# One pool for scores, value products and rows of reciprocals in an attention and gated-MLP kernel

## The chip, the cores and the metric

The kernel runs on one core of a Trainium2 chip. Its engines work side by side, each through its own list of instructions in a fixed order: TensorE (PE) multiplies matrices and is the only one that writes products, always into PSUM; VectorE (DVE) and ScalarE (ACT) read PSUM and compute elementwise; GpSimd (POOL) computes elementwise in SBUF; SyncE (SP) issues the transfers. PSUM has eight banks of 512 fp32 values per partition, and these banks are what the change hands out anew. The metric is the device time of one execution in microseconds (us).

## The reference

The kernel computes an attention with normalised queries and keys, and then a gated MLP over its result. There are 8 images, 12 heads, 448 positions and 64 values per head.

```python
q_n, k_n = rmsnorm(q, g_q), rmsnorm(k, g_k)
scores = q_n @ k_n.T / 8;  attn = exp(scores - max);  attn /= sum + 1e-9
x = (attn @ v)                                   # [8, 448, 768]
h = gelu_tanh(x @ w_in);  u, v = h[..., :512], h[..., 512:]
v_s = w_sg @ (layernorm(v) * g_ln) + b_sg        # mixes the 448 positions
out = x + (u * v_s) @ w_out
```

## The kernel before, in words

**Tiling.** Two heads form a pair, so an image has 6 pairs and the whole run has 48. Two pairs form a unit with one tile of queries and keys. Every factor of a product is held as a high and a low fp16 (or rounded fp32) part, and three products take the place of one.

**Scores (`scores`, L409).** A unit has 896 rows per head, cut into 7 tiles `s` of 128 rows, so a pair has three and a half. A tile has two banks, one per head, and comes from the pool `ps_s`, which holds two such tiles (`NS = 2`). TensorE fills it with six matmuls (twelve for the tile that the two pairs share, in half rows), L423. DVE takes the row maximum `nm` (L426), and ACT the two exponentials `ex` with their sums (L429), each of them an ACTIVATE and a read of the accumulator. With the second exponential the tile is free. The high part (ACT, L432) and the low part (DVE, L433) of the result go through a transposing transfer into `at`. The exact reciprocals of the sums are made in `recips`.

**Value product (`pv`, L445).** For each pair, `recip_row` (L392) first spreads the reciprocals over a row: 16 small matmuls into a tile `row` of the pool `ps_v`, which has a single bank (`NV = 1`), and a copy of it to SBUF by ACT (L406). Then 21 matmuls (L454, L459) build the product in the next tile `pv` of the same single bank, DVE multiplies it by the row in place (L461), ACT takes the high part `xh` (L464), and DVE the low part `xl` (L465), which is the last reader. So in `ps_v` the row's copy frees the bank for the product, and `xl` frees it for the next pair's row.

**MLP (`moe`, L489).** It runs one image behind, at lower priority. `mv` (L522, L525) makes the half that is normalised, `mu` (L580) the other half, `ms` (L608, L615) mixes positions, and `mo` (L647 to L659) adds the result to x. All their tiles come from `ps_m`, which has three banks (`NM = 3`). The gelus of a half run one after the other in a `cluster` (L471), since the gelu's table must be loaded (L475) and the exponential's restored afterwards (L484). Until a cluster runs, its tiles keep their banks, except those that ACT copies to SBUF first: `VC = (3,)` names the `mv` tile that is copied (L528, not in the first and last image), and `UC = (0, 1)` the two `mu` tiles (L585). The MLP of an image can start when its last pair's `xh` is there, and its remaining part is drained when the next one starts, one image later.

**Order.** The program is written as generators whose steps are interleaved with numbers (`SC`, `SV`, `M0`, `M1`, `MR`, `ML`), and with a priority per step; a scheduler then fixes the order on each engine, and which of a pool's slots a new tile takes (the one that it finds free, not strictly the next in turn). No order is decided on the chip.

Of the kernel before, what the change touches and what calls it, by code (L numbers as in the profile page):

```python
# [8 lines left out]
F32 = mybir.dt.float32  # L9
# [20 lines left out]

I0, WD = 5, 6

VC, UC = (3,), (0, 1)

SC, SV = 7, 3

NS, NV, NM = 2, 1, 3
NQK, NVR, RAWB = 2, 2, 3
NAT, NAH, NQT, NVH, HLB, GV = 3, 2, 2, 2, 3, 3
NOT, NX, NEX = 2, 12, 2  # L40
# [6 lines left out]
def kernel(  # L47
# [15 lines left out]
    B, H, S, D = q.shape  # L63
    P = 128
# [22 lines left out]
    sml = ctx.enter_context(tc.tile_pool(name="sml", bufs=4))  # L87
    xp = ctx.enter_context(tc.tile_pool(name="xp", bufs=NX))
    ps_s = ctx.enter_context(tc.tile_pool(name="ps_s", bufs=NS, space=bass.MemoryType.PSUM))
    ps_v = ctx.enter_context(tc.tile_pool(name="ps_v", bufs=NV, space=bass.MemoryType.PSUM))  # L90
    ps_m = ctx.enter_context(tc.tile_pool(name="ps_m", bufs=NM, space=bass.MemoryType.PSUM))
    mlp = None

# [295 lines left out]
        V.tensor_copy(out=rh, in_=y)  # L389
        V.tensor_tensor(out=rl, in0=y, in1=rh, op=ALU.subtract)  # L390

    def recip_row(i):  # L392

        u, j = divmod(i, NG)
        cs = slice(0, C4) if j == 0 else slice(CM, C7)
        rh, rl = U[u]["r", j]
        ps = ps_v.tile([P, 512], F32, name="row", tag="pv")[:, 0:S]
        for n, t in enumerate(range(cs.start, cs.stop)):
            ks, o = (slice(0, P), t * P - j * S) if t != CM else ((lo, SM), (hi, 0))[j]
            for rx in (rh, rl):  # L400
                for h in range(2):
                    w = ks.stop - ks.start
                    mm(out=ps[h * HP:(h + 1) * HP, o:o + w], lhsT=rx[ks, 2 * n + h:2 * n + h + 1].broadcast_to([w, HP]),  # L403
                       rhs=ident_h[ks, ks], start=(n == 0 and rx is rh), stop=(n == CM and rx is rl), skip_group_check=True)
        row = att.tile([P, S], F32, name="row", bufs=1)
        A.activation(out=row, in_=ps, func=AF.Copy)  # L406
        return row
# [37 lines left out]
    def pv(i):  # L445
        r = R[i]
        vh, vl = r["vh"], r["vl"]
        o = i % NAT * S
        yield
        row = recip_row(i)  # L450
        ps = ps_v.tile([P, 512], F32, name="pv")[:, 0:S]
        parts = ((vh, 0), (vl, 0), (vh, C7))
        for k_, (vx, n) in enumerate(parts):
            mm(out=ps, lhsT=vx[:, CM:CM + 2].rearrange("p c d -> p (c d)"), rhs=at_all[:, n + CM, o:o + S],  # L454
               start=(k_ == 0), stop=False, skip_group_check=True)
        for c in range(CM):
            for vx, n in parts:
                for h in range(2):
                    mm(out=ps[h * HP:(h + 1) * HP], lhsT=vx[:, c + h * (C4 + 1)], rhs=at_all[:, n + c + h * C4, o:o + S],  # L459
                       start=False, stop=(c == CM - 1 and n == C7), skip_group_check=True)  # L460
        V.tensor_tensor(out=ps, in0=ps, in1=row, op=ALU.mult)  # L461
        xh = xp.tile([P, S], F16, name="xh")
        xl = xp.tile([P, S], F16, name="xl")
        A.activation(out=xh, in_=ps, func=AF.Copy)  # L464
        V.tensor_tensor(out=xl, in0=ps, in1=xh, op=ALU.subtract)  # L465
        XT[i] = (xh, xl)
        del R[i]
        yield
# [245 lines left out]
    for i in range(NI + 1):  # L714
# [30 lines left out]
        if i > 0:  # L745
            streams.append((pv(i - 1), SV))
# [60 lines left out]
```

## Time and profile before

| | |
|---|---|
| time, 3 runs | 1026.87, 1028.56 (median), 1028.88 us |
| profiled execution: span from first to last instruction | 1021.5 us |
| median less span (what lies around the span) | 7.1 us |
| PE, DVE, ACT busy | 826.5, 801.4, 739.6 us |
| granted TensorE clock, mean | 0.925 |

The profile gives for the profiled execution its span alone; the 7.1 us around it are the difference to the median. Busy time is the union of an engine's instructions. A row of a group reads: line, engine, operation, out<-in, shapes, count, then busy time in us and the mean of one in ns, then the idle time ahead of it and who ended it. A row of waits reads: who waited, for whom, us in total, times, longest. A row of the timeline or of the chain of waits begins with its start and its length in us.

### The profile page before, as it was taken

Reading aid. Unit: us, or ns where it says so; the run is one execution under the profiler, and the core shown is the slowest. Engines: PE = TensorE matmul, PEld = TensorE weight load, DVE = VectorE, ACT = ScalarE, POOL = GpSimd, SP = SyncE. Lnnn points to the kernel's source line nnn. Section 1 sums busy time; section 2 is a strip of 40 time slices with the busy share of each in tenths; the row PEclk is TensorE's granted clock in tenths of the full one; section 3 lists DMA queues with packets and bytes.
Section 4 is the critical chain, followed back from the end, with each engine's and each line's share of the span. In section 5 each row is a group of like instructions: output and inputs, shape, how many; then the busy total and the mean of one; then the engine's idle time right before and its main releaser. Section 6 shows DMA issues by size and latency. Waiting matters only on the chain.

```text
span 1021.5 us, 16315 instructions
## 1 busy us (share of the span) xinstructions
PE 826.5 (81%) x5700; PEld 423.3 (41%) x5700; DVE 801.4 (78%) x1476; ACT 739.6 (72%) x1449; POOL 385.4 (38%) x263
## 2 busy tenths in 40 slices
PE   0324467737788899789897999989997899999998
PEld 0111224312553346344453455434643365445546
DVE  5699998999979977888789977887789768776140
ACT  2766798766777878686886877688778877786241
POOL 1465820436734362341543146322453253004021
PEclk9986678868989999899999899999998999999999
DMA  6977677776498869786789749793797676844102
GB/s 158 229 197 174 143 179 164 170 171 120 114 189 192 183 137 194 162 202 127 136 202 190 169 105 200 177 206 84 161 203 167 126 149 158 163 91 102 36 1 63
DMA packets 448002, 155.68 MB, mean 152 GB/s; under 512 B 404336, under 2 KB 441776, under 8 KB 447920
## 3 DMA queue, kind: packets, MB, share of 16 engines
q1 hardware_dynamic: 447344, 154.18, 69.3%
q8 instruction: 45, 0.74, 0.3%
q10 hardware_dynamic: 576, 0.46, 0.2%
q14 instruction: 37, 0.30, 0.1%
HBM read 43.57 MB, written 11.01 MB: 53 GB/s over the span
## 4 chain that ended last, share of the span: by engine, by line
DVE 31%; PE 28%; ACT 16%; DMA 10%; issue 9%; POOL 3%; SPq 3%; ACTq 0%; DVEq 0%; POOLq 0%
DVE ahl L433 8%; DMA at<-ahl 5%; DVE nm L426 5%; ACT ex L429 5%; ACT ahl L432 3%; PE s L423 3%; PE pv L459 3%; DVE vl L375 2%; DMA vr<-in_v_dram 2%; DVE ss L314 2%; DVE vl L568 1%; ACT sqv L358 1%; DVE pv L461 1%; DMA raw<-in_moe_w_in_dram 1%; SPq L302 1%
## 5 line engine op out<-in xcount | busy, mean ns | idle before, releaser
L429 ACT ACTIVATE ex<-s,nm 128x448 f32<-128x448 f32 x336 | 209.4, 631 | 76.8 <-DVE nm L426 51.6
L433 DVE TENSOR_TENSOR ahl<-ex,ahl 128x896 f16<-128x896 f32 x168 | 213.4, 1272 | 56.8 <-ACT ahl L432 55.4
L423 PE MATMUL s<-qt 64*128 64x448 f16 (+1 forms) x1152 | 156.9, 389 | 88.7 <-ACT ex L429 62.4
L426 DVE TENSOR_REDUCE nm<-s 128x2 f32<-128x896 f32 x168 | 180.8, 1081 | 18.4 <-PE s L423 18.2
L432 ACT ACTIVATE ahl<-ex 128x896 f16<-128x896 f32 x168 | 159.7, 951 | 37.8 <-DMA at<-ahl 35.8
L335 POOL TENSOR_TENSOR qk<-qk,ny 128x896 f32<-128x896 f32 x46 | 85.7, 1885 | 139.1 <-DVE ny L125 109.2
L619 POOL TENSOR_TENSOR gt<-gt,u 128x448 f32<-128x448 f32 x32 | 39.1, 1224 | 239.8 <-DVE gt L618 181.7
L340 POOL TENSOR_TENSOR hl<-qk,hl 128x896 f16<-128x896 f32 x46 | 94.6, 2070 | 69.9 <-ACT hl L339 69.7
L423 PEld LDWEIGHTS <-qt 64*128 64x128 f16 (+1 forms) x1152 | 49.2, 102 | 163.9 <-issue 102.8
L459 PE MATMUL pv<-at,vh 128*64 128x448 f16 x576 | 91.8, 371 | 0.0
L580 PEld LDWEIGHTS <-wi 128*128 128x128 f16 x576 | 57.6, 104 | 72.6 <-issue 31.3
L334 POOL TENSOR_TENSOR qk<-qk,gg 128x896 f32<-128x896 f32 x23 | 50.2, 2181 | 80.4 <-ACT sqk L313 78.2
L403 PE MATMUL row<-ident_h,rh 128*64 128x128 f16 (+1 forms) x384 | 36.6, 241 | 39.9 <-DVE xl L465 30.4
L429 ACT ACTIVATION_READ_ACCUMULATOR ex<-s,nm 128x1 f32 x336 | 67.8, 202 | 0.0
L314 DVE TENSOR_REDUCE ss<-sqk 128x14 f32<-128x896 f32 x48 | 51.6, 1076 | 17.6 <-ACT sqk L313 17.6
L313 ACT ACTIVATE sqk<-qk 128x896 f32<-128x896 f32 x48 | 45.6, 951 | 18.6 <-DVE ss L314 10.3
L339 ACT ACTIVATE hl<-qk 128x896 f16<-128x896 f32 x48 | 44.6, 945 | 13.6 <-POOL qk L335 6.9
L459 PE MATMUL pv<-at,vl 128*64 128x448 f16 x288 | 53.2, 367 | 0.0
L375 DVE SCALAR_TENSOR_TENSOR vl<-vr,v_s,vh 128x512 f16<-128x512 f32 x48 | 49.7, 1039 | 1.3 <-ACT vh L374 1.0
L459 PEld LDWEIGHTS <-vh 128*64 128x64 f16 x576 | 33.7, 114 | 40.5 <-issue 23.4
L403 PEld LDWEIGHTS <-rh 128*64 128x64 f16 (+1 forms) x384 | 22.5, 117 | 61.9 <-DVE xl L465 34.6
L522 PEld LDWEIGHTS <-xh 128*128 128x128 f16 x288 | 25.9, 99 | 46.8 <-issue 13.0
(1100 smaller groups left out, 2063.7 us busy)
## 6 DMA issues: line engine op xcount, KB each, us to landing
out_dram<-ot SPq DMA_DIRECT2D x56, 192.0 KB, 3.0
vr<-in_v_dram SPq DMA_DIRECT2D x32, 192.0 KB, 3.4
raw<-in_moe_w_in_dram SPq DMA_DIRECT2D x12, 512.0 KB, 5.5
qk<-in_q_dram SPq DMA_DIRECT2D x47, 128.0 KB, 2.9
qk<-in_k_dram SPq DMA_DIRECT2D x47, 128.0 KB, 2.8
vr<-in_v_dram SPq DMA_DIRECT2D x32, 144.0 KB, 3.2
qk<-in_q_dram SPq DMA_DIRECT2D x47, 96.0 KB, 2.6
qk<-in_k_dram SPq DMA_DIRECT2D x47, 96.0 KB, 2.6
```

The source lines that it names most:

```text
L314: V.tensor_reduce(out=SS[u][:, x], in_=skv, axis=AX.X, op=ALU.add)
L335: E.tensor_tensor(out=qk, in0=qk, in1=r["rs"][:, x * SSW:(x + 1) * SSW].unsqueeze(2).broadcast_to([P, SSW, D]), op=ALU.mult)
L340: E.tensor_tensor(out=l_, in0=r["qk"][:, x], in1=h_, op=ALU.subtract)
L375: V.scalar_tensor_tensor(out=vl.rearrange("p c d -> p (c d)"), in0=vr, scalar=sc, in1=vf, op0=ALU.mult, op1=ALU.subtract)
L403: mm(out=ps[h * HP:(h + 1) * HP, o:o + w], lhsT=rx[ks, 2 * n + h:2 * n + h + 1].broadcast_to([w, HP]), rhs=ident_h[ks, ks], start=(n == 0 ...
L423: mm(out=ps[r_, h, 0:S], lhsT=qt[hs, qx, t * P + r_.start:t * P + r_.stop], rhs=qt[hs, kx, j * S:(j + 1) * S], start=(m == 0), stop=(m == 2))
L426: V.tensor_reduce(out=nm, in_=ps[:, :, 0:S], axis=AX.X, op=ALU.max, negate=True)
L429: A.activation(out=ex[:, h], in_=ps[:, h, 0:S], func=AF.Exp, bias=nm[:, h:h + 1], accum_out=sums[:, t, h:h + 1])
L432: A.activation(out=ahl[:, 0], in_=ex, func=AF.Copy)
L433: V.tensor_tensor(out=ahl[:, 1], in0=ex, in1=ahl[:, 0], op=ALU.subtract)
L459: mm(out=ps[h * HP:(h + 1) * HP], lhsT=vx[:, c + h * (C4 + 1)], rhs=at_all[:, n + c + h * C4, o:o + S], start=False, stop=(c == CM - 1 and ...
L580: done = mm(out=ps[:, 0:S], lhsT=ww[:, g, f * P:(f + 1) * P], rhs=xx, start=(n == 0), stop=(n == 17))
```

## The change

The pool `ps_v` goes. A pair's `pv` tile now comes from `ps_s` under the scores' tag, as a tile of two banks: the product in the first, the row of reciprocals in the second. `ps_s` still holds two tiles. The bank that `ps_v` had goes to `ps_m`, which now has four. The copies of the `mv` tile (`VC`, six images) and of the second `mu` tile (`UC`, eight images) go. Lines after L90 stand one to two lines higher in the changed kernel (L423 is L421 there, L429 is L427, L589 is L588).

```diff
-VC, UC = (3,), (0, 1)
+VC, UC = (), (0,)
-NS, NV, NM = 2, 1, 3
+NS, NM = 2, 4
-    ps_v = ctx.enter_context(tc.tile_pool(name="ps_v", bufs=NV, space=bass.MemoryType.PSUM))
-    def recip_row(i):
+    def recip_row(i, ps):
         ...
-        ps = ps_v.tile([P, 512], F32, name="row", tag="pv")[:, 0:S]
         ...
-        row = recip_row(i)
-        ps = ps_v.tile([P, 512], F32, name="pv")[:, 0:S]
+        ps2 = ps_s.tile([P, 2, 512], F32, name="pv", tag="s")
+        ps = ps2[:, 0, 0:S]
+        row = recip_row(i, ps2[:, 1, 0:S])
```

The scheduler makes a new order of it on every engine. Three places follow; numbers behind a name tell one tile from the next, and "..." stands for matmuls that only repeat the row above and for weight loads.

**TensorE, between the last matmuls of one image's MLP and the first of the next image's (fifth MLP to sixth).** Before, the last `mo` matmuls, the score tiles and the first `mv` matmuls stand mixed:

```order
L659 MATMUL mo__7903<-wo_h_259,gl_7537 128x384
L403 MATMUL row_8168<-ident_h_89,rh_8089 64x64
...
L659 MATMUL mo__7903<-wo_h_259,gh_7493 128x384
L659 MATMUL mo__7903<-wo_l_260,gh_7493 128x384
L659 MATMUL mo__7903<-wo_h_259,gl_7639 128x384
...
L423 MATMUL s_8214<-qt_7714 128x448
...
L423 MATMUL s_8230<-qt_7714 64x448
...
L525 MATMUL mv__8289<-wi_256,xh_7096 64x256
```

In the changed kernel six score tiles and a whole pair's row and product stand there with no MLP matmul among them:

```order
L658 MATMUL mo__7857<-wo_h_256,gl_7594 128x384
L421 MATMUL s_7702<-qt_7146 128x448
...
L421 MATMUL s_7741<-qt_7146 128x448
...
L401 MATMUL pv_7777<-ident_h_86,rh_7650 64x64
...
L421 MATMUL s_7838<-qt_7146 128x448
...
L453 MATMUL pv_7777<-at_100,vh_7421 128x448
...
L421 MATMUL s_7881<-qt_7146 64x448
...
L421 MATMUL s_7947<-qt_7146 128x448
...
L421 MATMUL s_7963<-qt_7146 128x448
L131 MATMUL psc_8069<-vpart_7942,ones_79 128x2
...
L524 MATMUL mv__8241<-wi_253,xh_7054 64x256
```

What moved: two score tiles with MLP work on both sides became six tiles and a product in a row. Of the two slots, `pv_7777` has one from its first row matmul on, and `s_7741`, `s_7838` and `s_7881` follow one another in the other.

**ACT in the same stretch of the changed kernel**, from the first tile's exponentials to the last tile's (two exponentials are one row with x2):

```order
L427 ACTIVATE ex_7711,sums_7701<-s_7702,nm_7709 128x448 x2
L427 ACTIVATE ex_7750,sums_7701<-s_7741,nm_7748 128x448 x2
L404 ACTIVATE row_7794<-pv_7777 128x448
L427 ACTIVATE ex_7847,sums_7701<-s_7838,nm_7845 128x448 x2
L373 ACTIVATE vh_7934<-vr1_95,v_s_6756 128x512
L463 ACTIVATE xh_7818<-pv_7777 128x448
L427 ACTIVATE ex_7896,sums_7701<-s_7881,nm_7894 128x448 x2
L357 ACTIVATE sqv_7945,vpart_7942<-vr1_95 128x1536
L338 ACTIVATE hl_8050<-qk_7158 128x2x7x64
L427 ACTIVATE ex_7956,sums_7701<-s_7947,nm_7954 128x448 x2
L312 ACTIVATE sqk_8213<-qk_7681 128x896
L427 ACTIVATE ex_7972,sums_7701<-s_7963,nm_7970 128x448 x2
```

Four splits `ahl` and a second `hl` stand between these rows as well. ACT has all of its usual work for these tiles there, in a stretch in which TensorE has no MLP work.

**ACT, the first image's cluster of the `u` half.** Before, it stands in one piece:

```order
L475 ACT_TABLE_LOAD
L589 ACTIVATE u_1764<-mu__2030,hs_1099 128x448
L589 ACTIVATE u_1761<-u_1761,hs_1099 128x448
L589 ACTIVATE u_1762<-u_1762,hs_1099 128x448
L589 ACTIVATE u_1763<-mu__1977,hs_1099 128x448
L484 ACT_TABLE_LOAD
```

In the changed kernel exponentials have come between, and each change of table is a load:

```order
L474 ACT_TABLE_LOAD
L427 ACT_TABLE_LOAD
L427 ACTIVATE ex_1850,sums_1840<-s_1841,nm_1848 128x448 x2
...
L588 ACT_TABLE_LOAD
L588 ACTIVATE u_1754<-mu__2018,hs_1092 128x448
L588 ACTIVATE u_1752<-mu__1881,hs_1092 128x448
...
L427 ACT_TABLE_LOAD
L427 ACTIVATE ex_1981,sums_1840<-s_1972,nm_1979 128x448 x2
...
L588 ACT_TABLE_LOAD
L588 ACTIVATE u_1751<-u_1751,hs_1092 128x448
L588 ACTIVATE u_1753<-mu__1965,hs_1092 128x448
L483 ACT_TABLE_LOAD
```

What moved: the cluster has six table loads where it had two. The clusters of the other images stand in one piece in both.

## The prediction

> **What bounds the kernel now.** First the busy time of each engine by stage, then who waits inside the long middle stage, then one pair's timeline. Columns of the stage table: stretch, its length, busy time of PE, PE's weight loads, DVE, ACT and POOL, granted TensorE clock, DMA share, GB/s.
>
> ```profile
> 0.00:120.00 120.00, 35.31 (x247) 14.81 (x251) 97.89 (x156) 71.82 (x145) 63.00 (x47) 0.84 0.75 183
> 120.00:330.00 210.00, 152.53 (x1008) 75.12 (x1001) 189.14 (x346) 162.93 (x310) 92.84 (x59) 0.82 0.73 161
> 330.00:930.00 600.00, 552.24 (x3893) 278.23 (x3891) 492.59 (x926) 470.15 (x935) 214.27 (x141) 0.97 0.75 160
> 930.00:1022.00 92.00, 86.45 (x559) 55.12 (x559) 21.78 (x51) 34.72 (x62) 15.32 (x17) 1.00 0.19 46
> ```
>
> Up to 330 us DVE is the fullest engine (189.1 of 210 us). From 330 to 930 us, where two thirds of the pairs run, it is TensorE: 552.2 of 600 us, so 47.8 us idle. The tail is TensorE's too. No TensorE work goes with the change, so the middle can win at most those 47.8 us, and it loses whatever new idle time TensorE gets. Its waits there, and below them those over the whole run:
>
> ```profile
> PE s L423 <- ACT ex L429: 11.2, 13, 1.7
> PE row L403 <- DVE xl L465: 7.5, 5, 3.3
> PE pv L454 <- ACT row L406: 4.5, 4, 2.1
> PE ms__8822 L608 <- ACT u L589: 2.7, 1, 2.7
> PE mu__8508 L580 <- ACT vg L508: 2.5, 1, 2.5
> ...
> PE row L403 <- DVE xl L465: 30.4, 11, 8.9
> PE pv L454 <- ACT row L406: 5.6, 6, 2.1
> ```
>
> Waits for PSUM by the attention are 11.2 + 7.5 + 4.5 = 23.2 us of the 47.8. The score pool is not short today: each wait for `ex` averages 11.2 / 13 = 0.9 us. One pair (`s` tile, row, copy, product, its three readers):
>
> ```profile
> 576.12 0.74 PE L423 MATMUL s<-qt 64*128 64x448 f16 x6
> 578.04 0.25 PE L403 MATMUL row<-ident_h,rh 128*64 128x128 f16 x2
> 579.97 0.54 ACT L406 ACTIVATE row<-row 128x448 f32<-128x448 f32 x1
> 583.15 0.36 PE L454 MATMUL pv<-at,vh 128*128 128x448 f16 x1
> 587.38 0.63 DVE L461 TENSOR_TENSOR pv<-pv,row 128x448 f32<-128x448 f32 x1
> 590.57 0.62 DVE L465 TENSOR_TENSOR xl<-pv,xh 128x448 f16<-128x448 f32 x1
> ```
>
> From the first row matmul to the end of `xl` are 591.2 - 578.0 = 13.2 us. Today that occupies a bank of its own; in the change it occupies one of the scores' two slots.
>
> **The change part by part.** *Copies and tables.* Gone are six copies of 128x256 and eight of 128x448; added are four table loads in the first image's cluster, by the order.
>
> ```profile
> L528 ACT ACTIVATE vg<-mv__8289 x1: 366/366/366, 761.4 to 761.4; 128x256 f32<-128x256 f32 x1
> L585 ACT ACTIVATE u<-mu__5928 x1: 544/544/544, 575.1 to 575.1; 128x448 f32<-128x448 f32 x1
> L475 ACT ACT_TABLE_LOAD x18 | 23.1, 1283 | 16.2 <-PE mv__10601 L522 8.9 <-PE mv__10824 L522 2.2 <-PE mu__10958 L580 1.9
> ```
>
> 6 x 0.37 + 8 x 0.54 = 6.5 us go, 4 x 1.28 = 5.1 us come. ACT is idle a fifth of the time, which hides both: 0. Without that cover it would be -1.4.
>
> *A fourth MLP bank.* Before, three `mv` tiles wait in three banks with the fourth copied out; after, four wait in four. When the gelus start, every bank is taken in both, so the waits `mu <- vg` and `ms <- u` stay. Only `mo` gets a bank to spare, and no wait of the middle stage of any size names it. 0; at best the two waits quoted, 5.2 us.
>
> *The row's own bank.* The product no longer waits for the row's copy, nor the row for the last pair's `xl`: -4.5 - 7.5 = -12 in the middle. Of the early remainder (30.4 + 5.6 - 12.0 = 24.0) I take a tenth, TensorE not being the bound there: -2. Bounds 0 and -24. The copy itself still comes ahead of the multiplication and is now one reader among DVE's and ACT's others.
>
> *Two slots for three and a half score tiles and a product per pair.* The built program shows which slot each tile takes, so one can read off how much TensorE work stands between a tile's last matmul and the matmul that takes the slot over. That work must last longer than the readers. Their durations, with those of what else ACT does between:
>
> ```profile
> L426 DVE TENSOR_REDUCE nm<-s 128x2 f32<-128x896 f32 x168 | 180.8, 1081 | 18.4 <-PE s L423 18.2
> L429 ACT ACTIVATE ex<-s,nm 128x448 f32<-128x448 f32 x336 | 209.4, 631 | 76.8 <-DVE nm L426 51.6
> L429 ACT ACTIVATION_READ_ACCUMULATOR ex<-s,nm 128x1 f32 x336 | 67.8, 202 | 0.0
> L432 ACT ACTIVATE ahl<-ex 128x896 f16<-128x896 f32 x168 | 159.7, 951 | 37.8 <-DMA at<-ahl 35.8
> L433 DVE TENSOR_TENSOR ahl<-ex,ahl 128x896 f16<-128x896 f32 x168 | 213.4, 1272 | 56.8 <-ACT ahl L432 55.4
> L313 ACT ACTIVATE sqk<-qk 128x896 f32<-128x896 f32 x48 | 45.6, 951 | 18.6 <-DVE ss L314 10.3
> L339 ACT ACTIVATE hl<-qk 128x896 f16<-128x896 f32 x48 | 44.6, 945 | 13.6 <-POOL qk L335 6.9
> L358 ACT ACTIVATE sqv<-vr 128x1536 bf16<-128x1536 f32 x16 | 23.7, 1482 | 6.4 <-DMA vr<-in_v_dram 4.9 <-DVE ss L314 1.1 <-DVE nx L322 0.4
> L374 ACT ACTIVATE vh<-vr,v_s 128x512 f16<-128x512 f32 x48 | 33.8, 714 | 7.1 <-PE pv L459 6.5 <-DVE v_s L141 0.6
> L461 DVE TENSOR_TENSOR pv<-pv,row 128x448 f32<-128x448 f32 x48 | 30.0, 624 | 16.5 <-PE pv L459 16.4
> L464 ACT ACTIVATE xh<-pv 128x448 f16<-128x448 f32 x48 | 25.9, 539 | 20.0 <-DVE pv L461 19.9
> L465 DVE TENSOR_TENSOR xl<-pv,xh 128x448 f16<-128x448 f32 x48 | 29.4, 612 | 1.5 <-ACT xh L464 1.5
> ...
> 568.15 0.57 PE pv L454 x3
> 568.71 1.82 PE pv L459 x18
> 619.97 2.18 PE mo__6416 L659 x12
> 624.79 0.70 PE row L403 x16
> ```
>
> With nothing in their way the readers of a score tile need 1.08 + 2 x (0.63 + 0.20) = 2.75 us, those of a product 0.62 + 0.54 + 0.61 = 1.78 us. By the order of before, no tile of the middle has less than that as cover. By the new order 31 have, and 22 of them stand in five stretches, one at each passage from one image's MLP to the next, in which TensorE has no MLP matmul left: 4, 6, 4, 6 and 4 score tiles with a row and a product. The second of the long ones is the stretch shown above. Its seven slots are taken over after 1.42, 1.42, 0.74, 0.70, 2.39, 1.48 and 0.74 us of TensorE work (0.74 a score tile, 1.48 the shared one, 0.70 the row, 2.39 the product, 0.7 the four `mo` matmuls left at 2.18 / 12 each), against 1.78, 2.75, 2.75, 2.75, 2.75, 1.78 and 2.75 needed: 8.4 us short. The five together are 24.5 us short, by the bare durations: the floor. With one other instruction of the length of `ahl` on DVE (1.27 us) ahead of a score tile's readers and two ahead of a product's, 4.0 and 4.3 us, they are 63.6 us short: the ceiling. (In the pair above, the product ends at 583.15 + 2.39 = 585.5 and `xl` at 591.2, 5.7 us later, with TensorE busy meanwhile and in no hurry.)
>
> A second count lies between. From the first tile's exponentials to the last tile's ACT has, in the long stretch, 10 x 0.83 + 4 x 0.95 (`ahl`) + 2 x 0.95 (`hl`) + 0.95 (`sqk`) + 1.68 (`sqv` and its accumulator, taken as 0.19) + 0.54 (the row) + 0.54 (`xh`) + 0.71 (`vh`) = 18.4 us, TensorE 7.5 us: 10.9 idle. The five make 43 us. ACT may enter a stretch ahead by about the 2.75 us of a tile's readers, five times: 43 - 14 = 29. I take **+30**, near this count.
>
> Outside these stretches nine tiles are 9.5 us short by bare durations, and 29.7 us is the ceiling; MLP matmuls stand near them, so I take +8.
>
> *The clock after idle time.* A wait of TensorE already costs more than its length: after 1.5 us of it the eighteen matmuls of one tile took 6.3 us, at a clock of 0.53, where the same eighteen take 3.4.
>
> ```profile
> 561.80 0.53 PE L580 MATMUL mu__5814<-xh,wi 128*128 128x448 f16 x1 [1.54 <-ACT vg L508]
> 557.00:568.00 11.00, 9.06 (x48) 3.60 (x43) 10.54 (x25) 10.37 (x18) 2.21 (x2) 0.53 0.74 178
> ...
> 561.80 6.34 PE mu__5814 L580 x18
> 683.78 3.43 PE mu__7295 L580 x18
> ```
>
> That is 2.9 us. One such dip at each of the five stretches would cost 14; I take half, **+7**, bounds 0 and 14, since the matmuls there are few. The Trainium skill, "TensorE: Matmul & The Clock Gate", Part 1, says that the clock falls to half after about one idle window of 3.4 us and returns after a busy one. That rule speaks against the change, since every stretch without MLP work is a row of short idle times; the trace agrees on the half rate (0.53) but shows it around a wait of 1.5 us. By the rule each stretch would bring its dip, and the sum would be +38.
>
> **Sum.** 0 + 0 - 14 + 30 + 8 + 7 = +31. Span 1021.5 + 31 = 1052.5; with the 7.1 us around it **1060 us**, 3% more.
>
> **The rivals.** *(B) The scores become slot-bound throughout.* If the readers queue at DVE and ACT as they do now, the ceilings hold: 63.6 + 29.7 + 14 - 14 = +93, 1122 us. For it: DVE is busy 82% and ACT 78% of the middle. Against: while TensorE stands still their queues empty. It decides from the point where ACT or DVE has more than one foreign instruction ahead of a slot's readers.
>
> *(C) Faster.* The mechanism: TensorE reaches each stretch late, with ACT and DVE idle ahead of it, and the stretch is no longer than the idle time that TensorE has today in the same image (47.8 us over five and a half images). It decides if the stretches replace that idle time in place of adding to it: then the 23.2 us of slot waits go, and a tenth to a half of the early 24. -2 to -12 there, -12 to -23 here: -14 to -35, some 1004 us at -25. Against it: the floor of 24.5 us holds even with ACT and DVE idle.
>
> *(D) No change worth the name.* The floor, no dips, and nothing outside: +24.5, less 14, and 5 from the MLP banks: +5; a little more gain early makes it 0, 1029 us.
>
> In all of these the first 330 us may shift by 10 us either way, since the product now holds a slot through the long waits for DVE there; that is taken into the range alone.
>
> **How the numbers follow.** Forecast 0.50 (its own range 1036 to 1088), B 0.12, C 0.23, D 0.15. 0.2% is 2 us, about what a measurement of this kernel tells from none. D gives 0.08 to no change, 0.05 to slower, 0.02 to faster: faster 0.25, same 0.08, slower 0.67. The range 1008 to 1090 leaves out most of B and the lower half of C.
>
> **What would show it.** In the changed kernel: TensorE idle in the middle near 80 us; a larger `s <- ex` and a new `s <- xl` in its waits, near 40 us together, at five places some 110 us apart; no `pv <- row` wait; a granted clock there below 0.97; six table loads in the first `u` cluster. I am wrong if TensorE's idle time does not grow, or if it grows outside these five places.

## The result, and the profile after

| | before | change |
|---|---|---|
| time, median | 1028.72 us (4 runs, 1026.87 to 1031.21) | 1112.84 us (4 runs, 1110.07 to 1116.32) |
| ratio | 1 | 1.0843, 95% interval 1.0794 to 1.0891 |
| profiled execution, span | 1021.5 us | 1114.1 us |
| granted TensorE clock, mean | 0.925 | 0.876 |

The change makes the kernel 8.4% slower: 84 us, where 31 were forecast; the time lies above the range. The two profiled executions differ by 92.6 us, some 8 more than the medians. Runs for which time and span are both known have 1.7 to 2.5 us around the span, so the profiled execution of before took about 1023.4 us, and most of the 7.1 us that the section on the kernel before puts around the span are the distance of that execution from the median. The profiled execution of the change is the slowest of its four. The breakdowns below go by the profiles, and their total is too large by these 8 us. The stage table of the changed kernel, with the columns of the prediction's first fence:

```profile
0.00:120.00 120.00, 37.11 (x215) 14.62 (x215) 95.80 (x149) 67.70 (x136) 72.01 (x51) 0.79 0.74 180
120.00:330.00 210.00, 149.13 (x940) 68.63 (x940) 177.13 (x326) 158.15 (x293) 88.42 (x55) 0.78 0.66 154
330.00:930.00 600.00, 501.99 (x3450) 258.18 (x3451) 452.93 (x823) 420.19 (x819) 195.57 (x129) 0.89 0.66 144
930.00:1114.00 184.00, 160.96 (x1097) 86.09 (x1094) 96.03 (x180) 100.29 (x194) 30.69 (x29) 0.98 0.39 85
```

From 330 to 930 us TensorE ends 3450 matmuls where it ended 3893, and DVE and ACT are less busy too. No engine is fuller there than before; the time has gone into waits. What TensorE waits for in that stretch of the changed kernel (who, for whom, us in total, times, longest), and below "..." the same over the whole run, with the largest of the kernel before as the last row:

```profile
PE s L421 <- DVE xl L464: 24.4, 10, 5.3
PE pv L401 <- ACT ex L427: 18.7, 8, 4.0
PE psc L131 <- ACT sqv L357: 10.6, 5, 4.4
PE s L421 <- ACT ex L427: 6.6, 7, 1.6
PE pv L453 <- ACT row L404: 3.3, 4, 1.0
...
PE s L421 <- ACT ex L427: 42.9, 22, 5.2
PE pv L401 <- ACT ex L427: 42.7, 18, 7.3
PE s L421 <- DVE xl L464: 39.5, 15, 8.4
PE pv L453 <- ACT row L404: 6.2, 8, 1.0
...
PE s L423 <- ACT ex L429: 62.4, 30, 7.7
```

Two of these waits did not exist before: a score tile waits for the last reader of a product (`s <- xl`), and a product's row waits for the exponentials of a score tile (`pv L401 <- ex`). Over the run they are 39.5 + 42.7 = 82 us. But `s <- ex` fell from 62.4 to 42.9 us, and `row <- xl`, 30.4 us before, is gone. Together with `pv <- row` these waits grew from 98.4 to 131.3 us, by 33 us only.

For the comparison of kernels with other spans I cut each run at work instead of at times: *early* ends with the `xl` of the 13th pair, *middle* with that of the 47th (34 pairs), and the *tail* is the rest, to the end of the span. The middle of before and of the change, as rows of the stage table:

```profile
334.90:942.50 607.60, 559.84 (x3962) 284.39 (x3961) 496.47 (x929) 475.25 (x947) 214.62 (x144) 0.97 0.75 158
```

```profile
357.20:1049.40 692.20, 583.95 (x4056) 299.27 (x4055) 511.07 (x909) 478.17 (x941) 210.10 (x143) 0.90 0.64 140
```

So the 92.6 us are: early 357.2 - 334.9 = +22; middle +84.6, of it TensorE idle 108.2 - 47.8 = +60 and busy +24; tail 64.7 - 79.0 = -14. Of the 24, some 95 matmuls that were in the tail before are about 13 us at 0.141 us each, and the other 11 go with the slower clock (0.90 against 0.97). Of the 60, waits of scores, rows and products for a slot or for the row's copy are 38 (60.9 us against 23.2), and another 10.6 is `psc` (sums of squares that scale v) waiting for ACT's squares (0.2 us before). In the early part the same waits did not grow (75.2 us before, 70.5 in the change); TensorE is 18 us longer busy there, at a lower clock and with 40 more matmuls, and idle for 4 us more. DVE, the fullest engine of that part, is idle for 59 us where it was for 43. What makes it wait is not traced.

One of the five forecast stretches, the third, on TensorE ("..." stands for rows left out):

```profile
657.62 0.74 PE L421 MATMUL s<-qt 64*128 64x448 f16 x6 [0.16 <-ACT ex L427]
658.43 0.35 PE L453 MATMUL pv<-at,vh 128*128 128x448 f16 x1
...
660.91 0.76 PE L421 MATMUL s<-qt 64*64 64x448 f16 x12
665.22 1.49 PE L421 MATMUL s<-qt 64*128 64x448 f16 x12 [3.54 <-DVE xl L464]
669.88 0.32 PE L401 MATMUL pv<-ident_h,rh 128*64 128x128 f16 x2 [3.17 <-ACT ex L427]
```

The shared tile at 660.91 takes one slot, the product has the other, and TensorE stands still for 3.5 us until `xl` gives it back; two score tiles take both slots, and the next product waits 3.2 us for `ex`. That is the picture that the prediction drew. All five, with TensorE's busy time and the granted clock:

```profile
399.50:412.10 12.60, 7.33 (x72) 3.77 (x72) 7.48 (x17) 8.65 (x20) 0.00 (x0) 0.93 0.84 192
520.10:541.70 21.60, 12.74 (x105) 5.84 (x101) 12.63 (x18) 11.65 (x26) 0.00 (x0) 0.84 0.87 187
654.70:670.20 15.50, 8.55 (x87) 4.77 (x85) 12.11 (x18) 11.24 (x26) 0.00 (x0) 0.87 0.95 194
770.80:792.50 21.70, 12.61 (x87) 5.03 (x83) 13.53 (x19) 12.92 (x28) 0.00 (x0) 0.69 0.88 181
903.50:920.90 17.40, 9.66 (x86) 4.96 (x87) 12.14 (x19) 11.66 (x28) 0.00 (x0) 0.84 0.78 170
```

Length less busy time: 5.3 + 8.9 + 7.0 + 9.1 + 7.7 = 38 us. That leaves 108.2 - 38 = 70 us of idle time outside them, 22 more than before had in its whole middle. Of the 24.4 us of `s <- xl` above 22.5 lie in the five stretches; of the 18.7 us of `pv <- ex` only 7.2 do.

### The profile page after: what moved, and what is told of

The parts are those of the page before. It is cut to its first block, busy times and chain, and to the rows that moved or that the text cites. A ratio compares the mean times of both kernels' runs of the same rounds, so it can differ in the third digit from the quotient of the medians.

```text
span 1114.1 us, 16296 instructions
## 1 busy us (share of the span) xinstructions
PE 849.2 (76%) x5700; PEld 427.5 (38%) x5700; DVE 821.9 (74%) x1476; ACT 746.3 (67%) x1439; POOL 386.7 (35%) x263
## 4 chain that ended last, share of the span: by engine, by line
PE 33%; DVE 26%; ACT 16%; issue 9%; DMA 9%; SPq 3%; POOL 2%; ACTq 0%; DVEq 0%; POOLq 0%
DVE ahl L431 5%; DVE nm L424 5%; ACT ex L427 4%; PE pv L458 4%; DMA at<-ahl 3%; PE s L421 3%; DVE vl L374 2%; ACT ahl L430 2%; DMA vr<-in_v_dram 2%; DVE ss L313 2%; ACT L474 2%; PE pv L453 1%; DMA qk<-in_k_dram 1%; SPq L277 1%; POOL qk L334 1%
## 5 line engine op out<-in xcount | busy, mean ns | idle before, releaser
L427 ACT ACTIVATE ex<-s,nm 128x448 f32<-128x448 f32 x336 | 208.9, 628 | 125.3 <-DVE nm L424 116.5
L431 DVE TENSOR_TENSOR ahl<-ex,ahl 128x896 f16<-128x896 f32 x168 | 204.2, 1218 | 88.3 <-ACT ahl L430 87.9
L421 PE MATMUL s<-qt 64*128 64x448 f16 (+1 forms) x1152 | 148.2, 403 | 105.3 <-ACT ex L427 42.9
L339 POOL TENSOR_TENSOR hl<-qk,hl 128x896 f16<-128x896 f32 x46 | 97.3, 2126 | 295.7 <-ACT hl L338 295.6
L421 PEld LDWEIGHTS <-qt 64*128 64x128 f16 (+1 forms) x1152 | 46.8, 104 | 180.9 <-issue 70.6
L458 PE MATMUL pv<-at,vh 128*64 128x448 f16 x576 | 102.3, 412 | 0.0
L401 PE MATMUL pv<-ident_h,rh 128*64 128x128 f16 (+1 forms) x384 | 35.6, 239 | 53.3 <-ACT ex L427 42.7
L427 ACT ACTIVATION_READ_ACCUMULATOR ex<-s,nm 128x1 f32 x336 | 66.5, 198 | 0.0
L373 ACT ACTIVATE vh<-vr,v_s 128x512 f16<-128x512 f32 x48 | 34.3, 716 | 44.5 <-PE pv L458 44.5
L453 PE MATMUL pv<-at,vh 128*128 128x448 f16 x96 | 39.7, 413 | 30.5 <-DMA at<-ahl 15.8
L458 PE MATMUL pv<-at,vl 128*64 128x448 f16 x288 | 59.1, 408 | 0.0
L312 ACT ACTIVATE sqk<-qk 128x896 f32<-128x896 f32 x48 | 45.4, 945 | 16.1 <-DVE ss L313 8.5
L458 PEld LDWEIGHTS <-vh 128*64 128x64 f16 x576 | 36.6, 125 | 48.8 <-issue 35.4
L401 PEld LDWEIGHTS <-rh 128*64 128x64 f16 (+1 forms) x384 | 24.4, 117 | 72.8 <-issue 38.9
```

What stands on the lines that cost most here:

```text
L339: E.tensor_tensor(out=l_, in0=r["qk"][:, x], in1=h_, op=ALU.subtract)
L421: mm(out=ps[r_, h, 0:S], lhsT=qt[hs, qx, t * P + r_.start:t * P + r_.stop], rhs=qt[hs, kx, j * S:(j + 1) * S], start=(m == 0), stop=(m == 2))
L427: A.activation(out=ex[:, h], in_=ps[:, h, 0:S], func=AF.Exp, bias=nm[:, h:h + 1], accum_out=sums[:, t, h:h + 1])
L431: V.tensor_tensor(out=ahl[:, 1], in0=ex, in1=ahl[:, 0], op=ALU.subtract)
```

## The experiments

Three theories are tested. **S**: a product keeps one of the two slots for long, and the scores suffer in step with it. **O**: the loss is on the MLP's side, in the banks and the copies. **K**: taking turns costs by itself, however short the product's stay. The table gives what all runs showed; the ratio is to the kernel before on the same chip, and so the column to compare by. "Hold" is the mean time for which a product keeps its score slot, from the first matmul in it to the end of its last reader, in the 34 pairs of the middle, worked out from the starts and ends of these instructions.

| run | slots | MLP banks | median us | ratio (95%) | early / middle / tail us | idle TensorE, middle | hold |
|---|---|---|---|---|---|---|---|
| before | 2, product apart | 3 | 1028.7 | 1 | 335 / 607.6 / 79 | 48 | - |
| change | 2 shared | 4 | 1112.8 | 1.084 (1.079-1.089) | 357 / 692.2 / 65 | 108 | 11.9 |
| share_only | 2 shared | 3 | 1135.9 | 1.107 (1.103-1.111) | 358 / 707.0 / 66 | 110 | 13.6 |
| share_bank4 | 2 shared | 4 | 1107.6 | 1.080 (1.075-1.085) | 363 / 675.8 / 65 | 98 | 11.2 |
| after_sbuf | 2 shared | 4 | 1104.1 | 1.076 (1.073-1.080) | 351 / 683.5 / 66 | 95 | 10.8 |
| before_sbuf | 2, product apart | 3 | 1041.9 | 1.016 (1.011-1.021) | 343 / 613.3 / 80 | 51 | - |
| row_apart | 2 shared | 4, row in one | 1121.5 | 1.095 (1.089-1.100) | 358 / 697.3 / 69 | 111 | 7.5 |
| own_two | 2, product apart | 2 | 1046.8 | 1.021 (1.016-1.026) | 329 / 633.8 / 85 | 65 | - |
| before_m2 | 2, product apart | 2 | 1045.3 | 1.020 (1.015-1.024) | 328 / 630.9 / 85 | 69 | - |
| share3_m2 | 3 shared | 2 | 1033.7 | 1.009 (1.007-1.012) | 331 / 613.8 / 86 | 55 | 16.1 |
| single_slot | 1, product apart | 3 | 1219.6 | 1.191 (1.187-1.194) | 375 / 766.1 / 75 | 155 | - |
| spread8 | 2 shared | 4 | 1122.5 | 1.095 (1.093-1.098) | 358 / 698.3 / 65 | 109 | 12.7 |
| long_hold | 2 shared | 4 | 1146.6 | 1.120 (1.115-1.125) | 370 / 712.8 / 67 | 119 | 15.8 |
| share3_long | 3 shared | 2 | 1027.0 | 1.001 (0.998-1.004) | 336 / 608.7 / 79 | 62 | 21.0 |
| one_bank | 5 of one bank | 3 | 1035.5 | 1.010 (1.008-1.013) | 345 / 618.0 / 72 | 39 | |
| one_bank6 | 6 of one bank | 2 | 1086.6 | 1.060 (1.057-1.062) | 346 / 655.3 / 83 | 64 | |

### One part at a time: sharing, fourth bank, copies

Sharing alone, with the MLP as before and the eighth bank idle:

```diff
-NS, NV, NM = 2, 1, 3
+NS, NM = 2, 3
 # and the shared tile, as in the change; VC, UC = (3,), (0, 1) stay
```

> The product and the row share the scores' pool as in the change, but the MLP keeps three banks and all of its copies (the eighth bank lies idle). Theory S, the scores' slots: the whole loss is here, 1105 to 1120 us. Theory O, the MLP's side (no copies, a fourth bank that lets the MLP run dry early, a cluster split by exponentials): near the kernel before, 1025 to 1045 us.

Sharing and the fourth bank, with the copies of before:

```diff
 # against share_only; against the change it is VC, UC = (3,), (0, 1)
-NS, NM = 2, 3
+NS, NM = 2, 4
```

> The change with both sets of copies put back: shared slots, four MLP banks, copies of before. Theory S: 1100 to 1120 us, the bank moves it by less than 10 us either way. Theory O: if the fourth bank is what lets the MLP run dry, this is as slow as the change and the run without the bank is not; if the copies' absence matters, this is at least 20 us faster than the change.

Sharing alone costs 110 us by the medians, more than the whole change and 16 us above what S had forecast. The fourth bank gives 28 of them back (1.107 to 1.080), which the forecast had put at nothing, and taking the copies away after that moves nothing that the intervals separate (1.080 to 1.084). O falls: with the slots shared, the MLP's side of the change is a gain.

### A shorter hold

The multiplication writes into the row's tile in SBUF, so that the slot is free with it; and the same edit in the kernel before:

```diff
-        V.tensor_tensor(out=ps, in0=ps, in1=row, op=ALU.mult)
+        V.tensor_tensor(out=row, in0=ps, in1=row, op=ALU.mult)
+        ps = row
```

> The change, but the multiplication by the row writes to SBUF (into the row's own copy), so that the slot is free after the first of the three readers. By bare durations the slot is held 1.2 us less per pair, with the waits for ACT and DVE between the readers some 3 us less. Theory S: 20 to 60 us are won back, 1055 to 1090 us. Theory O: within 10 us of the change, 1103 to 1123 us.

> The kernel before with the same multiplication into SBUF, so that its single bank is free earlier for the next pair's row. The waits of the row for the last reader (30.4 us over the run, 7.5 of it in the middle) fall to those for the multiplication. Both theories: 1015 to 1028 us, if the row's copy, which now waits for the last reader of its SBUF tile, does not take the wait's place; else 1026 to 1035 us.

after_sbuf misses what S forecast and lies in the range of O; before_sbuf lies above both of its ranges. In the change `xl` ends 2.7 us after the multiplication, but the hold fell by 1.1 us only: from the slot's first row matmul to the product's first matmul it is now 6.5 us instead of 4.8. The middle fell by 8.7 us, while the same edit made before slower (1.016). The small gain speaks neither for S nor against it until one knows what a microsecond of hold is worth.

The other way to shorten it: the row goes to an MLP bank, and the product opens its score slot with its own first matmul.

```diff
+        row = recip_row(i, ps_m.tile([P, 512], F32, name="row", tag="mm")[:, 0:S])
         ps2 = ps_s.tile([P, 2, 512], F32, name="pv", tag="s")
         ps = ps2[:, 0, 0:S]
-        row = recip_row(i, ps2[:, 1, 0:S])
 # and VC, UC = (3,), (0, 1)
```

> The change with the copies put back and the row of reciprocals in a bank of the MLP's pool (four banks), so that a pair's product opens its slot of the scores' pool only with its first own matmul. In the run with four banks and the copies the slot is held 11.4 us per pair in the middle, 4.2 of it before the product's first matmul. Theory S (the loss is the time in which the product holds one of two slots): the hold falls to about 7 to 8 us and a third to a half of the loss goes, 1060 to 1085 us. Theory K (what costs is that a score tile must take turns with any third user at all, so that tiles stand behind one another in one slot, however short the hold): 1090 to 1110 us.

The hold fell from 11.9 to 7.5 us and the time did not fall at all. It lies above both forecasts, and 1.5 points above share_bank4 (1.080), from which this run differs by the row's bank alone. This seemed to be the end of S. TensorE's waits over the whole run, and below "..." the two largest of its middle:

```profile
PE s L421 <- ACT ex L427: 88.8, 28, 7.3
PE pv L453 <- DMA at<-ahl: 47.1, 8, 15.5
PE s L421 <- DVE xl L464: 35.2, 10, 9.7
PE row L401 <- DVE rh L388: 24.0, 16, 4.6
...
PE s L421 <- ACT ex L427: 39.7, 14, 5.8
PE pv L453 <- DMA at<-ahl: 13.0, 4, 5.1
```

The product's first matmul now waits 47.1 us for the transfers of its exponentials (15.8 in the change), 34.1 of them ahead of the middle and 13.0 in it (3.7 in the change). While its inputs are on their way the slot is empty, but the order has given it to the product, and no score tile may take it. The largest wait of the middle is that of the scores for `ex`, 39.7 us (9.1 in the change). From the tiles' banks in the built program and their times: in the middle the product holds its slot for 254 us, and for another 166 us it stands reserved and empty ahead of the product: 420 / 34 = 12.4 us a pair, close to the 11.9 us of hold in the change. But the change has some 65 us of reserved time as well, 13.8 us a pair with its hold, and share_bank4 has 78, 13.5 a pair. Counted alike, row_apart takes the slot for a little less than either, and yet its middle is 5 and 22 us longer than theirs. So reserved time can account for most of the gain that did not come, not for all; what the row costs in an MLP bank was not measured apart.

### Is it sharing, or the number of slots?

Two-bank slots leave room for three of them only with two MLP banks. So the control is the kernel before with two MLP banks and more copies, and beside it the product and its row in a two-bank tile of their own:

```diff
 # before_m2
-VC, UC = (3,), (0, 1)
-NS, NV, NM = 2, 1, 3
+VC, UC = (3, 0, 1), (0, 1, 2)
+NS, NV, NM = 2, 1, 2
 # own_two: before_m2, and
+        ps2 = ps_v.tile([P, 2, 512], F32, name="pv")
 # share3_m2: the change, with the same VC, UC and
-NS, NM = 2, 4
+NS, NM = 3, 2
```

> The kernel before with two MLP banks and the copies that they need (about 20 more copies, some 12 us of ACT): the control for the runs beside it. 1035 to 1065 us by both theories; the scores' pool is untouched.

> The product and the row have a two-bank slot of their own, the scores keep two slots, and the MLP has only two banks with more copies (mv: 3, 0, 1; mu: 0, 1, 2). Theory S: the attention is as free as before or freer, and the loss is what two MLP banks cost: within 10 us of the next run, which has the two banks and the old pool for row and product, and clearly below the change. Theory O (the order and the MLP's banks decide): 1080 us or more.

> Row and product share the scores' pool as in the change, but the pool has three slots; the MLP has two banks and the copies that they need. Theory S: the third slot takes the loss away, within 10 us of the run with a two-bank slot of its own. Theory K in its strong form (sharing as such costs, by the order in which tiles take slots): 30 us or more above that run.

With three slots, sharing is 1% faster than its control without sharing (1.009 against 1.020), although its product keeps a slot for 16.1 us, longer than in any of the two-slot runs then made. K in its plain form falls: taking turns costs nothing there. share3_m2 and own_two (1.021) both use all eight banks, so the gain is not that of a bank more. A product and row in one tile gain nothing by themselves (own_two against before_m2). `s <- xl`, 39.5 us in the change, is nearly gone in the run with three slots:

```profile
PE s L421 <- ACT ex L427: 54.6, 22, 9.1
PE pv L401 <- DVE xl L464: 17.3, 3, 7.7
PE s L421 <- DVE xl L464: 4.0, 4, 1.7
```

### What one slot is worth

The kernel before with a single score slot:

```diff
-NS, NV, NM = 2, 1, 3
+NS, NV, NM = 1, 1, 3
```

> The kernel before with one score slot instead of two (NS = 1), the product and row still in their own bank, three MLP banks, two banks idle. It prices score tiles standing behind one another in one slot all the time. If the loss of the change is the time in which a product has one of two slots (11.4 us of each 20.4 us of a pair in the middle, 56%), the loss here is about 85 / 0.56 = 150 us in the middle, and near 1180 us or more in all. If one slot is enough for the scores as long as nothing foreign stands in it, it stays within 30 us of the kernel before, 1060 us or less, and the loss of the change is then the score tiles' waiting for the product itself.

Its middle takes 766.1 us, 158.5 more than before (150 forecast); row of the stage table, below it TensorE's largest wait over the run (62.4 us before, with two):

```profile
374.90:1141.00 766.10, 611.08 (x4079) 302.57 (x4078) 515.42 (x923) 487.45 (x956) 212.04 (x143) 0.87 0.56 127
```

```profile
PE s L423 <- ACT ex L429: 168.7, 59, 7.1
```

Now both paces are known: 607.6 / 34 = 17.87 us a pair with two slots for the scores, 766.1 / 34 = 22.53 us with one. If scores go at the slower pace just while a product has a slot for h us, a pair takes T with h / 22.53 + (T - h) / 17.87 = 1, so T = 17.87 + 0.207 h, and the middle 607.6 + 7.0 h. Against the runs:

| run | hold h | middle by the rule | measured |
|---|---|---|---|
| after_sbuf | 10.8 | 683.4 | 683.5 |
| share_bank4 | 11.2 | 686.5 | 675.8 |
| change | 11.9 | 691.4 | 692.2 |
| spread8 | 12.7 | 696.5 | 698.3 |
| share_only | 13.6 | 703.3 | 707.0 |
| row_apart, hold alone | 7.5 | 660 | 697.3 |
| row_apart, with its reserved time | 12.4 | 694.5 | 697.3 |

In the five runs above row_apart the rule is off by 11 us at most, 1.6% of the middle, where the middle grew by 68 to 99 us. The holds are measured in the same runs, so this is an agreement and not yet a forecast, and an edit can move this kernel by as much through other causes (before_sbuf, 1.6%). row_apart fits if the time in which its slot stands reserved counts; but counted in the others as well, 62 to 78 us each, it puts the rule 13 to 16 us higher there, and above all of them. How reserved time counts stays open. By the rule some 17 of the 31 us that the fourth bank takes off the middle come from its hold, which is 2.4 us shorter.

### Are the five stretches the cause?

The change with the MLP's share of the interleaving lowered, which makes the stretches without MLP work longer (34 score tiles in them by the trace, 33 by the count made ahead, 24 in the change):

```diff
-WR, M0, M1, MR, ML = 3, 8, 7, 11, 11
+WR, M0, M1, MR, ML = 3, 8, 7, 8, 11
```

> The change with the MLP's share of the interleaving lowered from 11 to 8 steps a pair in the middle (MR). By its order the five stretches without MLP work become longer: 33 score tiles in them instead of 24. If these stretches are where the loss arises, the stall there grows in step, from about 38 us to about 52, and the time to some 1127 us. If the stretches are only where an attention that is paced by its two slots becomes visible, the time stays within 8 us of the change, the idle time only moving between the stretches and the rest.

The five stretches, and in the last row the middle:

```profile
385.90:411.30 25.40, 15.10 (x121) 6.96 (x120) 15.69 (x21) 16.88 (x38) 0.00 (x0) 0.77 0.92 184
514.80:544.70 29.90, 18.09 (x125) 8.19 (x125) 18.91 (x29) 18.43 (x41) 0.00 (x0) 0.69 0.78 181
641.60:669.70 28.10, 16.32 (x109) 7.54 (x108) 16.84 (x23) 16.75 (x38) 0.00 (x0) 0.75 0.77 176
768.40:795.40 27.00, 15.06 (x112) 7.47 (x110) 16.96 (x23) 16.81 (x36) 0.00 (x0) 0.81 0.78 182
893.80:917.80 24.00, 15.72 (x108) 6.43 (x111) 13.14 (x19) 13.91 (x29) 0.00 (x0) 0.64 0.89 177
358.00:1056.30 698.30, 589.33 (x4056) 304.67 (x4055) 500.02 (x908) 478.59 (x941) 208.33 (x143) 0.89 0.62 139
```

TensorE's idle time in them went from 38 to 54 us, as the first reading forecast (52). But its idle time in the whole middle stayed: 698.3 - 589.3 = 109.0 against 108.2. What the stretches gained, the rest lost, 70 to 55. So between these two profiles the stretches are where the waiting is seen, and lengthening them did not add to it. An account that fits: while MLP matmuls are at hand the order fills the scores' waits with them, and when they are used up the rest of the wait lies bare. In before and in share3_m2 no stretch of the middle has three score tiles and no MLP matmul; the runs with two shared slots and the one with a single slot have several.

The time does not settle it as cleanly. The run is 9.7 us slower than the change by the medians, 1.1% by the ratios, where the first reading had 14 and the second at most 8. Between the profiles it is 6.9 us, since that of the change is 3.5 us above its median, and 6 of these are in the middle, 5 of them TensorE busy at a lower clock. The hold is also 0.7 us longer, for which the rule above gives 5 us.

### The rule, forecast

A longer hold, at hardly any work: after `xl` four steps of one column, in turns on ACT and DVE, the last of which reads the product. The same in the kernel with three shared slots:

```diff
         V.tensor_tensor(out=xl, in0=ps, in1=xh, op=ALU.subtract)
+        z = xl[:, 0:1]
+        for n in range(2):
+            za, zd = ...
+            A.activation(out=za, in_=z, func=AF.Copy)
+            V.tensor_tensor(out=zd, in0=ps[:, 0:1], in1=za, op=ALU.add)
+            z = zd
```

> The change with the release of a product's slot put off: after the low part, four small steps of one column, ACT and DVE in turns, the last of which reads the product once more. By waits between the two engines of 0.9 and 1.4 us in the change, some 4 us more of holding, at little work. From the runs so far, a pair takes 17.87 us with two slots for the scores (607.6 / 34) and 22.53 us with one (766.1 / 34); if scores go at the slower pace exactly while a product holds a slot for h us, a pair takes 17.87 + 0.207 h, so every us of holding costs 7.0 us in the 34 pairs of the middle. With h at 16 instead of 11.9 the middle grows from 692 to about 720 us, and the whole run by 30 to 45 us, to some 1150. If the length of the hold does not matter, the time stays within 10 us of the change.

> The same four small steps in the kernel with three shared slots and two MLP banks, as the control: there two slots stay with the scores while a product holds the third. If it is the second slot that decides, the longer hold costs less than a third of what it costs in the change, 1034 to 1045 us; if the small steps cost by themselves (ACT and DVE, or the later start of what follows), it is as much as in the change.

The hold became 15.8 us, and the middle 712.8 us, where 720 was forecast and the rule gives 718 for the hold that came out; the whole run 1146.6 for "some 1150". Of three slots the product held one for 21.0 us, 5.0 longer than without the steps, and the middle did not grow (613.8 to 608.7; the whole run, 1027.0, is below the 1034 to 1045 that were forecast). Rows of the stage table for the middle of long_hold:

```profile
370.00:1082.80 712.80, 593.45 (x4056) 294.63 (x4055) 496.98 (x976) 493.89 (x1016) 213.19 (x143) 0.89 0.60 136
```

and of share3_long:

```profile
336.00:944.70 608.70, 546.86 (x3982) 287.14 (x3981) 482.36 (x985) 480.50 (x1020) 209.02 (x142) 0.95 0.71 155
```

So S stands after all, in this form: what costs is the time for which a product leaves one slot to the scores, and a microsecond of it costs 0.16 us (20.6 us of middle for 3.8 us more of hold in each of 34 pairs) to the 0.207 of the rule. That a slot reserved and empty costs as much as one that is held is argued from row_apart alone.

### Smaller slots

Scores, rows and products as one-bank tiles of one pool, with a row maximum for each head; five slots with the MLP of before, and six with two MLP banks and the copies of share3_m2:

```diff
-            ps = ps_s.tile([P, 2, 512], F32, name="s")
+            ps = [ps_s.tile([P, 512], F32, name="s", tag="s")[:, 0:S] for h in range(2)]
-            V.tensor_reduce(out=nm, in_=ps[:, :, 0:S], axis=AX.X, op=ALU.max, negate=True)
+            for h in range(2):
+                V.tensor_reduce(out=nm[:, h:h + 1], in_=ps[h], axis=AX.X, op=ALU.max, negate=True)
 # ... and row and product are a one-bank tile each, with the tag "s"
 # one_bank: NS, NM = 5, 3;  one_bank6: NS, NM = 6, 2
```

> The kernel before with scores, rows and products in one pool of five one-bank slots: each head's scores are a tile of their own with a row maximum of their own (336 of 448 values instead of 168 of 896; by the difference between 1081 ns for 896 and about 600 ns for 448 values elsewhere, some 10 to 20 us more work for DVE), row and product are one bank each; three MLP banks and the copies of before. As many banks as before for each side, but taken in turns. If it is the number of slots that decides, five slots lose little: 1015 to 1050 us. If taking turns between scores and products costs by itself, it is 1070 us or more.

> The same with six one-bank slots, two MLP banks, and the copies of the run with three shared two-bank slots and two MLP banks. If slots decide, it is at or below the 1034 us of that run, by at most 15 us; if the halved row maximum on DVE costs more than the finer slots give, 1040 to 1060 us.

Five shared slots of one bank lose 1%, as forecast if slots decide. Six of them lose 6%, which neither reading had. Three of TensorE's four largest waits over the run of one_bank6 (the fourth, 23.5 us, is a single wait for queries and keys):

```profile
PE pv L454 <- DMA at<-ahl: 29.6, 7, 17.8
PE row L402 <- DVE rh L388: 26.0, 11, 10.8
PE s L422 <- ACT ex L429: 20.4, 14, 7.0
```

The scores wait little (20.4 us, 54.6 in share3_m2), and the rows and products wait for their inputs. Why is open; the same six banks as three slots of two do 5% better. So the number of slots is not all that decides once they are of one bank.

No kernel of these runs beats the one before: share3_long is equal to it within its interval.

## Why the prediction was wrong

The direction was right, the size was not: +31 forecast, +84 by the medians and +92.6 between the two profiles, from which the last column is taken. By the prediction's own terms:

| term | forecast us | measured us |
|---|---|---|
| copies and tables | 0 | nothing that the intervals separate (share_bank4 to change) |
| fourth MLP bank | 0, at best -5 | -28 in the presence of sharing (share_only to share_bank4), contained in the rows below |
| five stretches | +30 | +38 |
| middle outside them, with the row's bank | 8 - 12 = -4 | +22 |
| first 330 us, with the row's bank | -2, and 10 either way | +22 |
| clock after idle time, middle | +7 | +11, as busy time that is left over |
| work moved from tail to middle | - | +13 and -14 |
| sum | +31 | +92 |

**What held.** TensorE's idle time in the stretches came out between floor and ceiling and near the second count; the five places lie 116 to 135 us apart, and from 330 to 930 us `s <- xl` and `s <- ex` are 24.4 + 6.6 = 31 us, where "near 40" was named, and TensorE is idle for 98 us, where "near 80" was. The four added table loads are there (before, L475 and L484 had 18 each):

```profile
L474 ACT ACT_TABLE_LOAD x18 | 23.1, 1283 | 5.0 <-PE mv__10539 L521 2.4 <-PE mu__10893 L579 1.9 <-PE mu__3337 L579 0.3
L483 ACT ACT_TABLE_LOAD x18 | 23.1, 1283 | 0.3
L427 ACT ACT_TABLE_LOAD x2 | 2.6, 1283 | 0.0
L588 ACT ACT_TABLE_LOAD x2 | 2.6, 1283 | 0.0
```

The clock fell in all five stretches (0.69 to 0.93). In the records of the granted clock 133 us of the middle are at half speed, 41 before, but TensorE's busy time grew by only some 11 us beyond the work that was moved there. The cost was compared, not isolated: no run changed the clock alone. The Trainium skill, "TensorE: Matmul & The Clock Gate", Part 1, has the clock fall to half after an idle window of about 3.4 us. The trace agrees on the half rate but not on the length: before, the clock fell at 895.1 us after one wait of 1.76 us, and in the change at 516.0 us after one of 1.54 us. The prediction's own example is read wrong in one point: it puts the slow 6.3 us of the `mu` tile at 561.80 down to the wait of 1.5 us just ahead of it, but the half rate begins at 557.2 us, after waits of 1.65 and 1.49 us that end at 554.76 and 556.60.

**The step that failed** is the part "Two slots for three and a half score tiles and a product per pair", in how it turned an order into a time. It compared, slot by slot, the TensorE work between two users with the readers' durations, and priced only the places where that work was too short. By this count the tiles outside the stretches are covered by MLP matmuls, so they cost 8, less 12 for the row's bank. Measured, TensorE's idle time outside them grew by 22, which the prediction had named as a sign of being wrong. But these matmuls are the same that fill such waits anywhere else, and there are only so many of them: the count took as free a cover that had to be paid for at the next passage or before. That this is how the waits spread is argued: 70 us of idle time outside the stretches bear it out, and the idle time of spread8. What single_slot and long_hold show is what should have been computed: a pace with two slots, a pace with one, and the share of time for which a product leaves only one. With hindsight, the 13.2 us of the pair that the prediction quotes, times 0.207, times 34, would be +93 in the middle, where +85 was measured. The 0.207 came from a run that was made later, and the closeness is in part luck: the mean of the 34 pairs of before, from the row's first matmul to the end of `xl`, is 9.1 us, which gives +64.

The two smaller failures go with it. **The row's own bank** was to give 12 + 2 us. `row <- xl` is gone, but the row's first matmul (now L401 in the product's tile) waits for `ex` instead, 42.7 us over the run against 30.4. And `pv <- row`, which was to vanish, is still there (6.2 us, 8 times; 5.6 us, 6 times before). **The first 330 us** were taken to move by 10 us at most, since TensorE is not the bound there. But every run with two shared slots has an early part of 351 to 370 us, and the others from 328 to 346, but for the single slot with 375. So the slots cost there too, although TensorE's waits for them did not grow in the change; how is open. The prediction also called the score pool "not short today" from the 11.2 us of `s <- ex` in the middle; over the whole run it is 62.4 us, 51.2 of them early.

**The rivals.** B gave 1122 us and was the nearest number. Its heading, that the scores become slot-bound throughout, is close to what the runs showed; its price was not got that way. It needed longer queues at DVE and ACT ahead of a slot's readers; the mean hold of a score tile fell, from 7.8 to 6.1 us, and the stretches cost 38 us, not 63.6. C and D rested on gains in the early part and from the row's bank that did not come.

The Trainium skill, "Perfetto Trace Analysis", Optimization Strategy, says that the same gap repeating on the engine that should be full can mean that SBUF or PSUM is short for the next tile. The trace agrees: 25 waits of `s` and `pv` for `xl` and `ex` in the stretch from 330 to 930 us, 49.7 us.

## What to carry to other kernels

When two kinds of tile share a pool of slots, price it by paces: how long a unit of work takes with all slots, how long with one fewer, and for what share of the time the other kind has a slot. Look also at the time for which the order reserves a slot that is still empty. An order in which other work stands in every gap does not show that the gaps are free: ask how much of that work there is, and look for the place where it runs out. A shorter hold won nothing in row_apart, where the product's slot then stood empty for longer, and with one slot more a longer hold cost nothing.

## What the runs showed that was not expected

- A product's first matmul waits for ACT's copy of the row wherever row and product are two banks of one tile (8, 6 and 4 such waits in the change, in own_two and in share3_m2), and only once in row_apart, where they are two tiles. In the change the product's first matmul never starts before the end of that copy, in row_apart it does in 24 of the 48 pairs. So two banks in one tile were not two independent places here.
- The fourth MLP bank, at best 5 us by the waits of before, was worth 28 us once the scores were short of slots.
- 192 small steps of one column on ACT and DVE cost nothing in the kernel with three slots; it ran 0.8% faster with them (1.009 to 1.001, intervals apart). They change the order on every engine; which of its moves gains is open.
